# A first weight loaded ahead of two value pairs, and one batch's q turned in two transfers, in an attention-and-maxout kernel

## The chip, the cores and the metric

The kernel runs on one core of one Trainium2 chip. The metric is device time in microseconds (us) of one execution; lower is better. "Span" is the stretch that the profile covers; it is about 1.8 us shorter than the device time of the same run (405.9 for 407.72). A ratio is the mean time of one kernel's fast runs over that of the other's of the same rounds, so it is not quite the ratio of the medians quoted beside it. Where a landing is given, it is the issue time plus the time to landing that the DMA view rounds to a tenth, so it is good to 0.05 us. A "stand" is a time in which PE stands idle.

## The reference, cut to what matters

```python
# batch 8, heads 8, sequence 1024, head_dim 64; k_proj 64
k_proj = einsum('ks,bhsd->bhkd', E, k);  v_proj = einsum('ks,bhsd->bhkd', F, v)
attn   = softmax(q @ k_proj.T / 8)
x      = (attn @ v_proj), heads side by side          # 8192 x 512
out    = max(x @ w1, x @ w2, x @ w3) @ w_out          # d_ff 768
```

## The kernel before

Each batch needs three loads (q, k, v; float32 in memory, cast to bf16 by the transfer), a projection of k and of v, q with head_dim on the partitions (`qT`), scores, the softmax, and `xT`, which the three weights multiply. The program order on each engine is fixed by hand. TensorE (PE) does the weight matmuls without a break, and the attention of the next batch lies between them.

Three places matter. The loads of the start, all on one queue in this order:

```python
load_q(LO, ...); load_kv(1, LO); load_q(HI, ...); load_kv(1, HI)   # q and k of batch 0
load_kv(2, slice(0, 2)); load_kv(2, slice(2, 4))                   # v pairs 0 and 1
...
load_kv(2, V2)                 # v pair 2
load_w(0, slice(0, 2))         # first half of the first weight
load_kv(2, V3)                 # v pair 3
...                            # rest of the weights, rest of q, w_out, then batch 1's q, k, v
```

The end of the start, and the first weight. `v_pair(g)` projects a pair of heads of v (8 matmuls), `x(g)` is its product with the attention (4 matmuls) and its scaling into `xT` on VectorE (DVE), `idle(n)` is n dummy matmuls; `z(g)` is the softmax sums of a pair and their inverse. (`at`, in the diff below, issues nothing: it only sets the time that the program keeps for choosing banks.)

```python
v_pair(1); z(2); z(3); x(1)
v_pair(2)
idle(2)
x(2)
idle(1)
...
for ct in range(4):            # up_first: 24 matmuls of the first weight, ct by ct
    for jt in range(6):
        up_mm(...); then((0, ct, jt))     # v_pair(3) after (0, 1, 2), x(3) after (0, 1, 5)
```

And batch 1's q. `qd` repacks q on DVE in four copies and turns it with one transposing transfer, on the queue of SyncE (SP). In the plan, `kproj`, `kt` and `vproj` project k, turn it, and project v; `sc` is the scores of a pair of heads and their exp, `za` its sums, its product with v and its scaling into `xT`; `qp` turns q on PE, `ld` issues a batch's loads:

```python
def qd(b):
    def f():
        q_p = att.tile([P, NPAIR, SI, 2, D], BF16, name="q_p", bufs=1)
        for g in range(NPAIR):
            copy("v", q_p[:, g]..., qkv[b][0][:, 2 * g:2 * g + 2], (), 0.43)
        qTs[b] = att.tile([P, NPAIR * SI, P], BF16, name="qT")
        last_T[b] = nc.sync.dma_start_transpose(out=qTs[b], in_=q_p...)
    return f

# plan of batch 0: (chunk, step): what follows that step; steps 0 to 5 are 12 weight matmuls each
(0, 6): [za(0, 1, *c1), sc(0, 3, *c1)],
(0, 7): [za(0, 2, *c1)],
(0, 8): [za(0, 3, *c1), qd(1)],
(1, 0): [kproj(1)],
(1, 1): [kt(1)],
(1, 2): [sc(1, 0), sc(1, 1), vproj(1), ld(2)],    # first scores of batch 1
(1, 3): [za(1, 0), sc(1, 2)],
(1, 4): [za(1, 1), sc(1, 3)],
(1, 5): [za(1, 2)],
(1, 7): [za(1, 3)],
```

The softmax here doesn't subtract the row's maximum and nothing guards it: scores larger than these inputs give would overflow.

## Time and profile before

| | before |
|---|---|
| device time, three timed runs | 409.61, 409.81, 410.21 us |
| device time of the profiled run | 407.72 us |
| PE busy, share of the span | 394.5 us, 97% |
| largest wait of PE | 2.7 us, for qT of batch 1 |

From the page of the kernel before: the busy line, the granted clock in 40 slices (tenths of full speed), and the chain of work that ended last, by engine.

```profile
PE 394.5 (97%) x2376; PEld 178.5 (44%) x2376; DVE 200.1 (49%) x309; ACT 191.1 (47%) x278; POOL 31.4 (8%) x44
PEclk9999999999999999999999999999999999999999
PE 87%; DMA 6%; ACT 2%; DVE 1%; POOL 1%; issue 1%; DVEq 0%; ACTq 0%; POOLq 0%
```

PE bounds the kernel, so only time in which PE stands can be won. The timeline of PE at the end of the start shows where it stands. Columns: start us, length us, engine, line, operation, output<-inputs, partitions, shape, count, and in brackets how long PE was idle before and what ended the idling.

```profile
17.25 0.30 PE L220 MATMUL banks<-pT,vp 64*64 64x256 bf16 x4
18.21 0.61 PE L422 MATMUL banks<-v_t,efT 128*128 128x128 bf16 x8 [0.65 <-DMA v_t<-in_v_dram]
18.65 0.59 PE L377 MATMUL banks<-warm 128*128 128x512 bf16 x2
19.20 0.30 PE L220 MATMUL banks<-pT,vp 64*64 64x256 bf16 x4
19.44 0.39 PE L377 MATMUL banks<-warm 128*128 128x512 bf16 x1
19.98 2.12 PE L497 MATMUL banks<-xT,w_sb 128*128 128x512 bf16 x9 [0.15 <-DMA w_sb<-in_moe_w_dram]
```

PE waits for v pair 2, works on it, fills up with dummies, and waits for the weight. The second place is batch 1's first scores, again in the timeline of PE; below it, the issues on the SP queue, where the 7.66 us are the time that the issue took.

```profile
52.63 2.75 PE L497 MATMUL banks<-xT,w_sb 128*128 128x512 bf16 x12
58.12 0.63 PE L200 MATMUL banks<-qT,kpT 64*64 64x512 bf16 x8 [2.73 <-DMA qT<-q_p]
...
43.77 0.35 SPq L606 DMA_DIRECT2D out_dram<-o_sb  x1
48.34 7.66 SPq L329 DMA_TRANSPOSE qT<-q_p  x1
```

### The profile page before, as it was taken

The numbers are of one execution on the slowest core, as the hardware profiler recorded it, in microseconds if no ns is written. First come the engines' busy times: TensorE is split into PE (matmuls) and PEld (weight loads), VectorE is DVE, ScalarE is ACT, GpSimd is POOL, SyncE is SP. The second block draws the span as 40 slices with busy tenths as digits, with TensorE's granted clock in tenths as the row PEclk, the third lists the DMA queues.
The fourth block names the chain that finished last, engine by engine and source line by source line (L and its number), as shares of the span: only waits on it lengthen the run. The fifth ranks groups of instructions, "written<-read, shape, count | busy, mean of one in ns | idle before, by whom it ended". The sixth has DMA issues, their size and how long they took to land.

```text
span 405.9 us, 5916 instructions
## 1 busy us (share of the span) xinstructions
PE 394.5 (97%) x2376; PEld 178.5 (44%) x2376; DVE 200.1 (49%) x309; ACT 191.1 (47%) x278; POOL 31.4 (8%) x44
## 2 busy tenths in 40 slices
PE   7899979999999999999999999999999999999996
PEld 3444433444444535444544445444544444444443
DVE  2447736462655537627353655626464363525251
ACT  2612429724763266555544555437535555432322
POOL 7440020002000100200200002000000000000000
PEclk9999999999999999999999999999999999999999
DMA  9999999948927994891798119950510202020202
GB/s 156 207 206 206 231 190 187 226 105 114 254 47 208 168 246 105 138 244 33 213 186 172 52 32 235 205 152 2 139 70 1 103 2 103 2 103 0 105 0 104
DMA packets 62635, 53.33 MB, mean 131 GB/s; under 512 B 30096, under 2 KB 58256, under 8 KB 62608
## 3 DMA queue, kind: packets, MB, share of 16 engines
q0 software_dynamic: 28512, 28.31, 43.7%
q1 hardware_dynamic: 33872, 24.25, 19.1%
q10 hardware_dynamic: 224, 0.39, 0.4%
q8 instruction: 18, 0.29, 0.3%
q14 instruction: 9, 0.07, 0.1%
HBM read 57.15 MB, written 16.78 MB: 182 GB/s over the span
## 4 chain that ended last, share of the span: by engine, by line
PE 87%; DMA 6%; ACT 2%; DVE 1%; POOL 1%; issue 1%; DVEq 0%; ACTq 0%; POOLq 0%
PE banks L497 58%; PE banks L592 19%; PE banks L220 4%; DMA w_sb<-in_moe_w_dram 3%; PE banks L284 3%; DMA qT<-q_p 2%; PE banks L200 2%; ACT pT L211 1%; ACT zl L233 1%; DVE xT L250 1%; ACT zi L239 1%; POOL v_t L147 1%; DMA out_dram<-o_sb 0%; DVE hs L507 0%; POOL k_t L147 0%
## 5 line engine op out<-in xcount | busy, mean ns | idle before, releaser
L497 PE MATMUL banks<-xT,w_sb 128*128 128x512 bf16 x1152 | 257.2, 379 | 0.2 <-DMA w_sb<-in_moe_w_dram 0.2
L497 PEld LDWEIGHTS <-w_sb 128*128 128x128 bf16 x1152 | 109.6, 98 | 136.5 <-issue 9.4
L557 DVE TENSOR_TENSOR m<-banks,h1s 128x512 f32<-128x512 f32 x90 | 62.0, 689 | 83.8 <-ACT h1s L553 52.5
L553 ACT COPY h1s<-banks 128x512 f32<-128x512 f32 x90 | 52.5, 583 | 90.0 <-PE banks L497 88.0
L592 PE MATMUL banks<-wout_sb,hT 128*128 128x512 bf16 x378 | 85.6, 379 | 0.1
L250 DVE TENSOR_TENSOR xT<-banks,zi 128x1024 bf16<-128x1024 f32 (+1 forms) x36 | 39.8, 1106 | 76.9 <-ACT zi L239 55.5
L507 DVE TENSOR_TENSOR hT<-banks,m 128x512 bf16<-128x512 f32 x90 | 62.3, 692 | 10.1 <-DVE m L557 0.5
L99 ACT COPY o_sb<-banks 128x512 f32<-128x512 f32 (+1 forms) x60 | 34.9, 581 | 52.9 <-PE banks L592 52.9
L592 PEld LDWEIGHTS <-hT 128*128 128x128 bf16 x378 | 36.0, 98 | 45.4 <-issue 2.8
L233 ACT ACTIVATE zl<-banks 128x1024 f32<-128x1024 f32 (+1 forms) x36 | 33.5, 931 | 29.5 <-PE banks L220 27.9
L211 ACT ACTIVATE pT<-banks 128x1024 bf16<-128x1024 f32 (+1 forms) x36 | 33.2, 931 | 13.5 <-PE banks L200 13.5
L239 ACT ACTIVATE zi<-zl 128x1024 f32<-128x1024 f32 (+1 forms) x36 | 34.6, 962 | 1.1
L189 POOL DMA_DIRECT2D q_t<-in_q_dram x7 | 6.2, 880 | 205.4 <-DMA qT<-q_p 142.9
L200 PE MATMUL banks<-qT,kpT 64*64 64x512 bf16 (+1 forms) x144 | 13.7, 358 | 3.2 <-DMA qT<-q_p 2.7
L220 PE MATMUL banks<-pT,ones 64*64 64x512 bf16 (+1 forms) x144 | 13.9, 375 | 0.7 <-DVE xT L250 0.3
L284 PEld LDWEIGHTS <-efT 128*64 128x64 bf16 x256 | 12.8, 110 | 4.0 <-issue 3.6
L220 PE MATMUL banks<-pT,vp 64*64 64x512 bf16 (+1 forms) x144 | 13.3, 355 | 0.1
L99 DVE CAST vp<-banks 64x256 bf16<-64x256 f32 (+1 forms) x18 | 7.1, 396 | 10.2 <-ACT vp L99 6.9
L220 PEld LDWEIGHTS <-ones 64*64 64x64 bf16 x144 | 4.5, 103 | 14.6 <-issue 13.5
L99 ACT CAST vp<-banks 64x256 bf16<-64x256 f32 x14 | 5.1, 365 | 12.0 <-PE banks L284 11.8
L377 PE MATMUL banks<-warm 128*128 128x512 bf16 x26 | 9.2, 480 | 1.2 <-DVE warm L170 1.2
L99 DVE COPY q_p<-q_t 128x1024 bf16<-128x1024 bf16 x28 | 10.0, 419 | 0.0
(46 smaller groups left out, 97.4 us busy)
## 6 DMA issues: line engine op xcount, KB each, us to landing
out_dram<-o_sb SPq DMA_DIRECT2D x30, 512.0 KB, 3.0
q_t<-in_q_dram POOLq DMA_DIRECT2D x7, 1024.0 KB, 9.5
k_t<-in_k_dram POOLq DMA_DIRECT2D x7, 1024.0 KB, 13.8
v_t<-in_v_dram POOLq DMA_DIRECT2D x7, 1024.0 KB, 18.5
w_sb<-in_moe_w_dram POOLq DMA_DIRECT2D x5, 384.0 KB, 12.3
k_t<-in_k_dram POOLq DMA_DIRECT2D x2, 512.0 KB, 8.8
v_t<-in_v_dram POOLq DMA_DIRECT2D x4, 256.0 KB, 11.5
wout_sb<-in_moe_w_out_dram POOLq DMA_DIRECT2D x1, 768.0 KB, 16.0
```

The lines of the kernel that those rows point to most:

```text
L99: done = {"v": nc.vector.tensor_copy, "s": nc.scalar.copy, "g": nc.gpsimd.tensor_copy}[eng](out=o, in_=i)
L211: nc.scalar.activation(out=pTs[b, g, lo], in_=t, func=AF.Exp, scale=scale)
L220: nc.tensor.matmul(out=t[hp * HALF:(hp + 1) * HALF, c, 0:nsi * HALF], lhsT=w(rows, hp), rhs=p[rows, hp, :], start=True, stop=True,)
L233: nc.scalar.activation(out=zl, in_=t, func=AF.Ln)
L239: nc.scalar.activation(out=zi, in_=zl, func=AF.Exp, scale=-1.0)
L250: nc.vector.tensor_tensor(out=xTs[b][:, g, lo:lo + nsi, :].rearrange("a (c s) p -> a c (s p)", c=2), in0=t, in1=zi, op=ALU.mult,)
L284: nc.tensor.matmul(out=t[hh * HALF:(hh + 1) * HALF, 0:width], lhsT=efT[:, si, (kv - 1) * KP:kv * KP], rhs=qkv[b][kv][:, heads[hh], si, :], ...
L497: nc.tensor.matmul(out=h, lhsT=w_sb[i][:, ct, jt * P:(jt + 1) * P], rhs=xTs[b][:, ct, ch * SPC:(ch + 1) * SPC, :], start=(ct == first), st ...
L507: nc.vector.tensor_tensor(out=o, in0=h, in1=other, op=ALU.max)
L553: nc.scalar.copy(out=h1s, in_=h[0][0])
L557: nc.vector.tensor_tensor(out=m12, in0=h[1][0], in1=h1s, op=ALU.max)
L592: nc.tensor.matmul(out=o_ps, lhsT=hTs[b, ch][:, jt, tt * P:(tt + 1) * P], rhs=wout_sb[:, jt, :], start=(jt == 0), stop=(jt == NJT - 1),)
```

## The change

It means to take both stands away. The first weight comes ahead of the last two v pairs, whose work then lies between weight matmuls. Batch 1's q is repacked one step sooner and turned in two halves, so that the first scores need wait for one half only. F's load also moves from the ACT to the SP queue, and batch 0's second q repacking moves by two matmuls.

```diff
-    nc.scalar.dma_start(out=ef_f[KP:P], in_=F)
+    nc.sync.dma_start(out=ef_f[KP:P], in_=F)
...
+    load_w(0, slice(0, 2))
     load_kv(2, V2)
-    load_w(0, slice(0, 2))
     load_kv(2, V3)
...
-    def qd(b):
+    def qd(b, parts=1):
...
+            n = NPAIR // parts
+            for lo in range(0, NPAIR, n):
+                for g in range(lo, lo + n):
+                    copy( ... )
+                last_T[b] = nc.sync.dma_start_transpose(
+                    out=qTs[b][:, lo * SI:(lo + n) * SI, :],
+                    in_=q_p[:, lo:lo + n].rearrange("p g si h d -> p (g si h d)"),
+                )
...
-    at(16.7)
-    v_pair(2)
-    idle(2)
-    x(2)
     idle(1)
-    at(18.4)
+    at(17.4)
...
-                (0, 7): [za(0, 2, *c1)],
-                (0, 8): [za(0, 3, *c1), qd(1)],
+                (0, 7): [qd(1, 2), za(0, 2, *c1)],
+                (0, 8): [za(0, 3, *c1)],
...
-                    (0, 1, 2): [lambda: v_pair(3), ld(1)],
-                    (0, 1, 5): [lambda: x(3)],
-                    (2, "a", 1): [qp(0, (0, 1), *c1)],
+                    (0, 0, 5): [lambda: v_pair(2)],
+                    (0, 1, 2): [lambda: x(2)],
+                    (0, 1, 5): [lambda: v_pair(3), ld(1)],
+                    (0, 2, 2): [lambda: x(3)],
+                    (2, "a", 2): [qp(0, (0, 1), *c1)],
```

More of the change, by code (lines that the diff above doesn't have):

```diff
@@ L317, in qp @@
         return f
-    def qd(b):
+    def qd(b, parts=1):
         def f():
             q_p = att.tile([P, NPAIR, SI, 2, D], BF16, name="q_p", bufs=1)
-            for g in range(NPAIR):
-                copy(
-                    "v", q_p[:, g].rearrange("p si h d -> p h si d"),
-                    qkv[b][0][:, 2 * g:2 * g + 2], (), 0.43,
-                )
-            qTs[b] = att.tile([P, NPAIR * SI, P], BF16, name="qT")
-            last_T[b] = nc.sync.dma_start_transpose(
-                out=qTs[b], in_=q_p.rearrange("p g si h d -> p (g si h d)")
-            )
+            qTs[b] = att.tile([P, NPAIR * SI, P], BF16, name="qT")
+            n = NPAIR // parts
+            for lo in range(0, NPAIR, n):
+                for g in range(lo, lo + n):
+                    copy(
+                        "v", q_p[:, g].rearrange("p si h d -> p h si d"),
+                        qkv[b][0][:, 2 * g:2 * g + 2], (), 0.43,
+                    )
+                last_T[b] = nc.sync.dma_start_transpose(
+                    out=qTs[b][:, lo * SI:(lo + n) * SI, :],
+                    in_=q_p[:, lo:lo + n].rearrange("p g si h d -> p (g si h d)"),
+                )
         return f
```

## The prediction

> **What bounds the kernel now.** TensorE: the page has it busy 394.5 of 405.9 us (97%) at a granted clock of 0.999; the chain of waits is 87% PE. The waits of PE are small: 2.7 us for qT of batch 1, 0.7 us for v_t, 0.2 us for w_sb, and about 2.7 us in the first microseconds, which the change does not touch. At most some 4 us are in reach.
>
> **Start.** In the timeline PE finishes the second value product near 17.5 us, waits 0.65 us for the third v pair (landed 18.15), does its matmuls, three dummies and a product, then waits for the first weight piece (issued 7.03, 12.9 to landing: 19.93). The POOL queue's landings come in order of issue, so swapping the two puts the weight at about 18.15 + 1.8 - 1.3 = 18.6 us and the v pair at 19.9. Six weight matmuls (0.22 us apart) fill 18.6 to 19.95; the value work then lies between weight matmuls. The first weight's 24 matmuls end at 25.6 us instead of 26.0, with perhaps 0.2 us of waiting for the last xT. The second weight lands at 24.96, the rest of q at 32.26, the last weight at 33.7, as before (same bytes ahead of them); the q transposes (before at 32.35, after waiting for a max) stand two matmuls later and meet q as it lands. Gain about 0.4 us, at most 0.8; the DMA is full here, which caps it.
>
> F moves from the ACT to the SP queue, issued 0.58 us later. The Trainium skill (Trainium Kernel Development and Optimization, Key Constraints) says all queues share the same 16 DMA engines and a further issuer saves only issue time; E and F landed at 5.4 and 6.3 us. I expect F within 0.4 us of that, hidden by the five dummies before the first k projection, which waits for k.
>
> **Batch 1's q.** Before: four copies on DVE, 46.89 to 48.31, one transfer issued at 48.34 (issue 7.66 us), landed 58.07; PE stood from 55.39 to 58.12. After: the copies follow the second o_sb copy, from about 43.3 (q landed 42.6); the first half's transfer starts near 44.1, the second near 48, landed by 54. The first scores need only the first half. PE arrives near 55.0, so the 2.73 us go entirely. The 1.42 us of copies delay xT of pairs 2 and 3 to about 45.4 and 46.7; they are needed near 46.3 and 47.8, and the banks come free in time.
>
> **What it collides with.** The first transfer now overlaps batch 1's k load (42.6 to 47.65). Before, v took 6.85 us beside the transfer instead of the 5.05 that k took. I estimate k 1 us later, 48.6, against PE's arrival at 48.5: a new wait of 0.1 to 0.5 us.
>
> **Sum.** 409.81 - 0.4 - 2.7 + 0.2 = about 406.9 us, 0.7% less. Range 405.9 to 408.4. Faster by over 2%: 0.01; within 2%: 0.98; slower by over 2%: 0.01.
>
> **Right if** the waits of PE for qT vanish, the first weight matmul starts near 18.6, the first qT transfer is issued near 44, and PE busy falls by only about 1 us while the span falls about 3.
>
> **Wrong if** (a) transfer and k load slow each other, so that PE waits 1 us or more at batch 1's k projection, or v arrives late at its projection near 55.5; (b) DVE waits for q_t at 43.3 and holds xT up; (c) the weight lands no earlier than 19.5; (d) the unmoved landings of weights, q or w_out absorb the start's gain: then about 407.3.

## The result, and the profile after

The kernel after takes 406.51 us (median of 4 runs, 406.15 to 406.83) against 409.9 (4 runs, 409.61 to 410.21): ratio 0.9917, 95% interval 0.99 to 0.9934. The forecast of 406.9 and its direction hold. The steps behind it do not, and the traces say so at once. The same lines of the page of the kernel after:

```profile
PE 391.0 (97%) x2330; PEld 178.2 (44%) x2374; DVE 199.9 (49%) x309; ACT 190.9 (47%) x278; POOL 31.6 (8%) x44
PEclk9999999999999999999999999999999999999999
PE 83%; DMA 10%; ACT 2%; issue 1%; POOL 1%; DVE 1%; ACTq 0%; POOLq 0%
```

The span is 405.1 us, only 0.8 less than in the trace before, though the timed runs differ by 3.4. (Part of the fall in PE busy is that the trace lacks some matmul records: 2330 for 2374 weight loads.) The end of the start, in the timeline of PE of the kernel after; the line of x2 has a record missing:

```profile
18.04 0.39 PE L380 MATMUL banks<-warm 128*128 128x512 bf16 x1
18.98 1.47 PE L496 MATMUL banks<-xT,w_sb 128*128 128x512 bf16 x6 [0.55 <-DMA w_sb<-in_moe_w_dram]
20.28 0.61 PE L425 MATMUL banks<-v_t,efT 128*128 128x128 bf16 x8
20.95 0.59 PE L496 MATMUL banks<-xT,w_sb 128*128 128x512 bf16 x2
21.47 0.30 PE L220 MATMUL banks<-pT,vp 64*64 64x256 bf16 x4
21.71 0.82 PE L496 MATMUL banks<-xT,w_sb 128*128 128x512 bf16 x3
22.57 0.61 PE L425 MATMUL banks<-v_t,efT 128*128 128x128 bf16 x8
```

The weight matmuls begin a microsecond sooner, and the value work lies among them as planned. Batch 1's scores and the SP queue of the kernel after:

```profile
52.86 2.75 PE L496 MATMUL banks<-xT,w_sb 128*128 128x512 bf16 x12
57.41 0.63 PE L200 MATMUL banks<-qT,kpT 64*64 64x512 bf16 x8 [1.80 <-DMA qT<-q_p]
...
43.91 0.36 SPq L605 DMA_DIRECT2D out_dram<-o_sb  x1
44.58 12.49 SPq L331 DMA_TRANSPOSE qT<-q_p  x2
```

The first half was issued 3.8 us sooner than the whole had been, yet it landed at 57.38, only 0.7 us sooner, and PE still stands for 1.80 us. So this pair of traces accounts for 0.8 us of the gain. The rest had to be found.

### The profile page after: what moved, and what is told of

It is laid out like the page before. It is cut to its first block, busy times and chain, and to the rows that moved or that the text cites. A ratio compares the mean times of both kernels' runs of the same rounds, so it can differ in the third digit from the quotient of the medians.

```text
span 405.1 us, 5869 instructions
## 1 busy us (share of the span) xinstructions
PE 391.0 (97%) x2330; PEld 178.2 (44%) x2374; DVE 199.9 (49%) x309; ACT 190.9 (47%) x278; POOL 31.6 (8%) x44
## 4 chain that ended last, share of the span: by engine, by line
PE 83%; DMA 10%; ACT 2%; issue 1%; POOL 1%; DVE 1%; ACTq 0%; POOLq 0%
PE banks L496 55%; PE banks L591 19%; PE banks L220 4%; DMA q_t<-in_q_dram 3%; DMA qT<-q_p 3%; DMA w_sb<-in_moe_w_dram 3%; PE banks L284 3%; PE banks L200 2%; ACT pT L211 1%; ACT zl L233 1%; DVE xT L250 1%; ACT zi L239 1%; DMA out_dram<-o_sb 0%; POOL k_t L147 0%; POOL q_t L152 0%
## 5 line engine op out<-in xcount | busy, mean ns | idle before, releaser
L284 PE MATMUL banks<-k_t,efT 128*64 128x256 bf16 (+1 forms) x144 | 8.7, 263 | 1.3 <-DMA k_t<-in_k_dram 1.2
```

Of the source, the lines that this page charges most:

```text
L284: nc.tensor.matmul(out=t[hh * HALF:(hh + 1) * HALF, 0:width], lhsT=efT[:, si, (kv - 1) * KP:kv * KP], rhs=qkv[b][kv][:, heads[hh], si, :], ...
```

## The experiments

All outputs were correct. Kernels ran beside eleven runs of the kernel before; their medians were 410.19 (chip of the first four kernels), 409.34 (next four) and 409.31 (last four).

**1. `a_before`: the kernel before, unchanged.**

> The kernel before, unchanged, to learn how far its profiled run of 407.7 us stands for its timed runs of 409.6 to 410.2. Theory A (the one trace of before is typical, the 2 us are the profile's own offset): ratio 1.000 within 0.002, and a new trace with a span near 406, PE waiting 2.7 us for qT and not at all for batch 1's k. Theory B (that trace was a quick execution; the DMA landings of the start vary by about a microsecond from run to run): a new trace with later landings than 9.7 us for the first k, and a longer span, near 408.

Five fast runs: 408.04, 408.06, 409.23, 409.28, 410.28; median 409.23, ratio 0.997 (0.9948 to 0.9992) against the very same program. So an interval can miss by 0.3%, and a difference under about 1 us needs a trace. The run that was profiled (513.58 us, clock 0.754) serves for nothing. The numbers lie in two groups about 1.2 us or more apart, and the first trace of before (407.72) belongs to the quicker one: Theory B, in its first half. The record gives each run's mean granted clock too: 0.998 and 0.999 in the two quick runs, 0.994 to 0.995 in the other three.

**2. `b_start`: the start part alone.** Edit: the load order, the start sequence, the `up_first` places and the later q step of the diff above; F and `qd` as before.

> The start alone: first weight loaded ahead, value pairs between its matmuls, first q step later; F still on the ACT queue, batch 1's q repacked as before. Theory A (prediction): 0.4 us less, ratio 0.999, as the start is held by landings. Theory B (the start is worth most of the 3.4 us, because the typical before stands longer there than its trace showed): 2 to 3 us less, ratio 0.993 to 0.995.

Median 409.80, ratio 0.999 (0.9973 to 1.0006). Theory B of this run falls. Whether it gives 0.4 us or nothing is settled below with twelve traces.

**3. `c_q`: the q part alone.** Edit: `qd(b, parts)` and the two lines of the plan.

> Batch 1's q alone: copies a step sooner, two transfers; start as before. Theory A (prediction): 2.5 us less, ratio 0.994, wait of PE for qT gone. Theory B (the trace after: the transfer moves hardly any packets while the k and v loads run and ends with the v load): qT wait falls by about 1 us only, a wait for k of about 1 us appears, total within 0.5 us of before, ratio 0.999 to 1.001.

Median of five fast runs 407.09, ratio 0.9922 (0.9906 to 0.9939), nearly the whole gain. Its trace is slow (418.7 us) and not used; run 9 repeats it.

**4. `d_f`: F on the SP queue alone.**

```diff
-    nc.scalar.dma_start(out=ef_f[KP:P], in_=F)
+    nc.sync.dma_start(out=ef_f[KP:P], in_=F)
```

> Only F's load moved to the SP queue. Prediction: nothing, ratio 1.000 within 0.001. Rival (in the trace after, the first k landed 0.6 us later than in that of before, and everything behind it too; F's move would be the cause): the first k lands 0.6 us later in this trace, and the time rises by 0.3 to 0.6 us.

Runs of 407.03, 407.22, 407.53 and of 409.20, 409.47, 409.50: two groups again, their means 2.1 us apart. The ratio, 0.9954, comes from how many runs fell in each, and with run 1 in mind I draw no gain from it. The rival falls: the first k landed at 9.81 us in this trace, against 9.71 in that of before and about 10.3 to 10.81 in the other fast traces with F on the ACT queue.

This trace, of a run of the slower group, shows what can separate the groups. The windows view, with windows laid on the edges of the clock records; columns: stretch, length, busy us of each engine (instructions), granted clock of PE, DMA share, GB/s. First `d_f`, then the first trace of before. The clock records of `d_f` begin and end at 7.16, 58.36, 61.77 and 406.52 us, whole multiples of 3.413 us apart; before has none between 5.56 and 404.92, and its edges are counted on from these two in the same steps.

```profile
54.95:58.36 3.41, 0.86 (x11) 0.24 (x8) 1.12 (x2) 0.00 (x0) 0.00 (x0) 1.00 1.22 338
58.36:61.77 3.41, 3.19 (x26) 1.72 (x20) 0.37 (x1) 0.73 (x2) 2.62 (x3) 0.50 0.44 47
61.77:65.18 3.41, 3.39 (x23) 1.26 (x22) 1.87 (x4) 2.98 (x4) 0.00 (x0) 1.00 1.17 181
```

```profile
53.35:56.76 3.41, 2.03 (x10) 0.81 (x9) 1.65 (x4) 0.59 (x1) 0.00 (x0) 1.00 1.29 222
56.76:60.17 3.41, 2.06 (x27) 1.21 (x27) 0.00 (x0) 0.38 (x2) 1.54 (x2) 1.00 0.61 202
```

In `d_f` the stand of 2.55 us fell into one window of 3.41 us, PE was busy for 0.86 us of it, and the clock was halved for the whole next window, 0.4 us after the scores began. In the first trace of before an edge, at 56.76, cut the stand of 2.73 us in two, PE was busy for 2.03 and 2.06 us of the windows, and the clock stayed. The Trainium skill describes this (TensorE: Matmul & The Clock Gate, Part 1: The HAM clock gate): the array's clock is halved after an idle window of 4096 cycles at 1.2 GHz, 3413 ns, and the window runs freely, not from the kernel's start. The trace agrees on both: the half-clock stretch lasts 3.41 us, and the edges stand elsewhere in every run. It differs in one point: the window need not be idle, busy for a quarter is little enough. The mean clock does not sort all runs, though: the two quickest of `d_f` (407.03 and 407.22) have 0.994 and 0.995, as the slow ones have. Where their clock dropped, and why it cost them nothing that shows, is not known.

The cost: from the start of the scores to the end of the program's fifth `h1s` copy on ScalarE (the second after the scores) takes 7.53 us in the trace of before, 9.11 in `d_f`, 9.04 in `b_start` (whose scores also ran at half clock) and 8.91 in `e_one` (run 6). A drop there costs about 1.5 us on top of the stand. The next run tests this by itself.

**5. `k_fill`: the stand filled with dummies.** The stand stays, the idling goes.

```diff
-                (1, 2): [sc(1, 0), sc(1, 1), vproj(1), ld(2)],
+                (1, 2): [lambda: idle(11), sc(1, 0), sc(1, 1), vproj(1), ld(2)],
```

> The kernel before with 11 dummy matmuls (about 2.4 us of PE time) set just before batch 1's first scores, where PE otherwise stands for qT; nothing else changed, and qT lands no sooner. Theory C (in most executions of before the granted clock halves for 3.41 us right after that stand, as the traces of d_f and b_start show and the first trace of before does not; that costs about 1.7 us more than the stand itself): 1.5 to 2 us less than before, about 408.2, the fast runs in one group rather than spread from 408.0 to 411.5, and a clock of 1.00 in the stretch after 58 us. Rival (the clock event is harmless, only the landing of qT counts): unchanged, or slower by up to 0.3 us, ratio 1.000 to 1.001.

All six runs lie between 408.07 and 408.40. The kernel before, in the same rounds: five runs from 407.65 to 408.42 and six from 409.34 to 410.26. In these rounds the mean clock sorts the runs of before exactly: 0.999 in the five, 0.994 to 0.996 in the six; in `k_fill` it is 0.999 or 1.000 in all but the profiled run, whose one drop lies in the start. So the slower group is gone and the quicker one is where it was: filling the stand with useless work wins what the clock drop cost, and no more. Its trace has no drop after the scores, which start at 58.44, and the 7.53 us are back:

```profile
56.38:59.79 3.41, 3.41 (x34) 1.72 (x32) 0.48 (x1) 0.00 (x0) 1.04 (x2) 1.00 0.80 244
59.79:63.21 3.42, 3.37 (x25) 1.39 (x21) 1.96 (x4) 2.87 (x5) 1.58 (x2) 1.00 0.84 101
```

Against the slower group's 409.7 the gain is 1.4 us, just short of the 1.5 to 2 forecast; against the mean of before it is 0.7 us (ratio 0.9983, 0.9962 to 1.0003), as half of those runs were quick.

**6. `e_one`: the kernel after, with one transfer.**

```diff
-                (0, 7): [qd(1, 2), za(0, 2, *c1)],
+                (0, 7): [qd(1), za(0, 2, *c1)],
```

> The kernel after, but batch 1's q turned in one transfer, still issued a step sooner. Theory (the transfer's 256-byte packets pass at about 150 a us while loads run, and only the end of the v load frees them; two halves bring nothing, since both landed within 1.8 us of each other): same as after, 406.5 within 0.5. Prediction's view (scores need only the first half, which lands early): 1 us or more slower than after.

My theory of that moment missed: median 409.68, ratio 1.0007 (0.9979 to 1.0035). Without the split nothing is left of the gain. PE and the SP queue in the trace of `e_one`:

```profile
58.65 1.07 PE L200 MATMUL banks<-qT,kpT 64*64 64x512 bf16 x8 [3.02 <-DMA qT<-q_p]
...
45.35 11.23 SPq L331 DMA_TRANSPOSE qT<-q_p  x1
```

Issued 3.0 us sooner than before, it landed at 58.65, if anything later (58.04 before), and the clock dropped. The reason is in the DMA view. Two queues of the kernel after from 50 to 52 us, q0 being the loads and q1 the transfer (packets, MB, share of 16 engines' time), then q1 of the kernel before from 56 to 57 us, when the loads had ended:

```profile
q0 software_dynamic: 303, 0.31, 91.0%
q1 hardware_dynamic: 304, 0.08, 29.9%
```

```profile
q1 hardware_dynamic: 1132, 0.29, 128.0%
```

Beside a load the two queues pass as many packets, 304 to 303 in 2 us. The Trainium skill (DMA: Bandwidth & Descriptors, Queues, rings and completion order) states that an engine goes round its queues a packet at a time; a packet there holds several descriptors, and whether the packets of the profile are the same is not shown. The equal counts agree with equal turns, and here the turns are unequal in size: the transfer's packets hold 256 bytes, the load's 1024. So it passes 152 packets a us, and 1132 alone. The whole transfer is 1 MB, 4096 packets; most of it goes through once batch 1's v load is done. An early transfer takes turns from the loads: v landed between 55.56 and 56.22 us in the six traces with an early issue, and between 54.44 and 55.68 in the six with a late one (`a_before` and the slow trace of `c_q` left out), on average about 1 us later. An early issue also starts the packets less early than it seems. In the trace of after the transfer was issued at 44.58 but moved its first 256-byte packet at 49.46, against 48.34 and 51.69 in before: 3.8 us sooner in issue, 2.2 in packets. The output write issued just ahead of it on the same queue moved its own packets from 47.41 to 50.16; that the transfer waited behind it was not tested. The engines are full, so what the transfer gains by starting sooner, the load ahead of the fast stretch gives back.

**7. `g_after_late`: the kernel after, batch 1's attention one step later.** PE then reaches the scores when qT is there.

```diff
-                (1, 0): [kproj(1)],
-                (1, 1): [kt(1)],
-                (1, 2): [sc(1, 0), sc(1, 1), vproj(1), ld(2)],
-                (1, 3): [za(1, 0), sc(1, 2)],
-                (1, 4): [za(1, 1), sc(1, 3)],
-                (1, 5): [za(1, 2)],
+                (1, 1): [kproj(1)],
+                (1, 2): [kt(1)],
+                (1, 3): [sc(1, 0), sc(1, 1), vproj(1), ld(2)],
+                (1, 4): [za(1, 0), sc(1, 2)],
+                (1, 5): [za(1, 1), sc(1, 3)],
+                (1, 6): [za(1, 2)],
```

> The kernel after, with batch 1's k projection, k turn, scores and all but the last of its exp-and-value steps one matmul step (2.6 us) later, so that PE reaches the scores after qT has landed near 57.4. Theory: no wait for qT at all, another 1.5 to 1.8 us less than after, about 404.8. Rival (the wait only moves to the later steps, to xT or to the v projection): same as after.

Median 405.40 (404.88 to 407.11), ratio 0.9918 (0.9894 to 0.9942), the lowest of all medians. PE in its trace no longer waits for qT:

```profile
58.31 0.63 PE L200 MATMUL banks<-qT,kpT 64*64 64x512 bf16 x8
```

A wait of 0.4 us for a bank that VectorE frees late has come up at a following output step, so some 1.4 of the 1.8 us should remain; the medians differ by 1.0 to 1.1, less than the 1.5 to 1.8 that was forecast.

**8. `h_before_late`: the kernel before, with the same later steps and nothing else.**

> The kernel before with only those steps of batch 1 one matmul step later: same transfer at the same time, start unchanged. Theory C: the wait of 2.7 us falls to nearly nothing and no clock drop follows, so 4 us less than before, about 405.7; it would beat the kernel after without any of its changes. Rival: the wait moves elsewhere; 408 or more.

Median 406.62 (406.51 to 407.19), ratio 0.9944 (0.9923 to 0.9965). PE waits 0.22 us for qT and the clock stays at full speed. The expected 405.7 was 0.9 us too hopeful; the new 0.4 us wait for a bank is part of the difference. A move in the plan, without a transfer touched, thus brings a time close to that of the kernel after. In the same rounds the mean of `g_after_late` is still 1.1 us lower (405.62 and 406.70); of this 0.5 us stands at the start of the scores in the two traces (58.31 and 58.80), the wait for qT included; the rest is not explained.

**9. `c_q_again`: the q part alone, for a fast trace.**

> The q part alone once more, for a trace in the fast state (the first fell in the slow one). Theory D (two halves let the first scores start when the first half lands, about 1 us before a single transfer would, which shortens PE's stand to under 2 us, and the granted clock then does not drop): qT wait 1.5 to 2 us against 2.5 to 3.0, no half-clock stretch near 58 us, about 407. Prediction's view (the wait goes entirely, no other effect): qT wait under 0.3 us.

Runs of 405.98 to 407.86, median 407.28, ratio 0.9948 (0.9927 to 0.9969). Line of PE's waits from 14 to 70 us in its trace:

```profile
PE banks L200 <- DMA qT<-q_p: 1.4, 1, 1.4
```

No half-clock stretch follows in this trace (one of the three other runs, 407.47, has a mean clock of 0.994, so its clock dropped somewhere). The prediction's view (under 0.3 us) falls; Theory D holds, with a wait a little under its 1.5 to 2 us.

**10. `f_split_late`: the kernel before, with two transfers at the old step.**

```diff
-                (0, 8): [za(0, 3, *c1), qd(1)],
+                (0, 8): [za(0, 3, *c1), qd(1, 2)],
```

> The kernel before with batch 1's q turned in two transfers, but at the old step. Theory D, the split is what counts: the first half lands near 57.2 instead of 58.3, the wait is about 1.5 to 2 us, mostly no clock drop, 1.5 to 3 us less than before. Rival, the earlier issue counts as much (the first half needs the 2.3 us of packet time that it gained beside the loads): first half lands at 58 or later, wait as before, clock drop, within 0.7 us of before.

Median 406.68 (405.50 to 406.77), ratio 0.9932 (0.9915 to 0.9949): the gain of the whole change. Its PE and SP lines, and the window of the clock in which the stand falls:

```profile
57.28 0.63 PE L200 MATMUL banks<-qT,kpT 64*64 64x512 bf16 x8 [1.35 <-DMA qT<-q_p]
...
48.09 8.78 SPq L331 DMA_TRANSPOSE qT<-q_p  x2
```

```profile
54.21:57.62 3.41, 2.06 (x16) 0.83 (x14) 1.38 (x2) 0.59 (x1) 0.00 (x0) 1.00 1.29 191
```

The first half landed at 57.19 and the second at 58.98, 1.8 us apart, which is 2048 packets at 1132 a us. The scores start on the first half, the stand is 1.35 us, and a stand that short leaves PE busy enough (2.06 us) even where one window holds all of it.

**11. `a_after`: the kernel after again.**

> The kernel after again, beside the others: 406.5 within 0.6, no half-clock stretch near 58 us, qT wait 1 to 2 us. If its start part is worth what was predicted, 0.4 us less than the q part alone; if nothing, equal to it within 0.3.

Median 406.40 (405.74 to 407.10), ratio 0.9931 (0.9916 to 0.9946); wait 1.4 us for qT, no clock drop. It equals `f_split_late` of the same rounds (means 406.40 and 406.48). Of the two forecasts for the start neither fits: the q part alone, `c_q_again`, has a mean of 407.10, 0.7 us more, but from four runs spread over 1.9 us; the first `c_q` had nearly the ratio of the whole change (0.9922 and 0.9917). The timed runs leave a few tenths open, so the start is judged by traces below.

**12. `m_spread`: as `g_after_late`, the last two steps further on.**

```diff
-                (1, 6): [za(1, 2)],
-                (1, 7): [za(1, 3)],
+                (1, 7): [za(1, 2)],
+                (1, 8): [za(1, 3)],
```

> The kernel after with batch 1's steps later as in g_after_late, and the last two exp-and-value steps one further step on, so that the first output step does not wait 0.4 us for a bank that VectorE frees late. If that wait is all that g lost: 0.3 to 0.4 us less than g, about 405.0. If the last xT comes too late for batch 1's first matmuls instead: 0.5 us or more above g.

Median 405.69 (405.54 to 406.06), ratio 0.9915 (0.99 to 0.993), 0.7 us under `a_after` of the same rounds by the means (405.74 and 406.40). Against g, of another submission, no difference can be claimed: the expected 0.3 to 0.4 us is below what separates submissions. In its trace the 0.4 us wait is gone, but PE waits 0.7 us for the last `xT` at the first matmuls that need it (77.12 us): the wait has moved.

**The start part, from twelve traces.** PE's first weight matmul, and the start of the first `o_sb` copy on DVE, which all twelve share after the start; us.

```
start as before   first weight  first o_sb     start changed    first weight  first o_sb
before               19.98        40.85        after               18.98        41.00
d_f                  20.29        40.91        b_start             19.72        41.60
k_fill               20.99        41.60        e_one               19.22        41.10
h_before_late        20.64        41.45        g_after_late        19.38        41.25
c_q_again            20.60        41.43        a_after             19.32        41.20
f_split_late         20.13        41.27        m_spread            19.56        41.44
mean                 20.44        41.25        mean                19.36        41.27
```

The first weight starts 1.1 us sooner, and 20 us later nothing is left; the first k landed at the same time in both columns on average (10.3 us). With six traces a side that spread by up to 0.75 us, a gain below some 0.3 us (an estimate from this spread) could still hide. The gain is lost inside the first weight: from its first matmul to the last of the six `hs` copies that take its results away takes 6.52 us in the trace of before and 7.78 in that of after (starts of the two). In between now lie a further v pair (8 matmuls, 0.45 us), a further product with its pause (0.33 us), a pause of 0.20 us before the last v pair's matmuls, and one of 0.28 us for the last xT: 1.26 us together, the whole difference. Before, PE did that pair and that product while it waited for the weight anyway; they cost nothing there. What is won in landing is about what the moved work costs in its new place.

Also, chance moves this point by up to 0.75 us between runs of equal kernels: compare before with `k_fill`, equal up to there. It follows the loads: the first k landed at 9.71 in the one and at 10.81 in the other.

## Why the prediction was right or wrong, point by point

- **The time (406.9 predicted, 406.51 measured), the direction and the range** were right, the number by luck: in the q part too large a cut of the wait and a clock cost that was left out nearly cancelled, at 2.7 us predicted. Of the "right if" list the main point failed, as the wait for qT did not vanish.
- **"The 2.73 us go entirely": wrong.** The stand is 1.80, 1.42 and 1.39 us in the three fast traces with the q part as changed, so 0.9 to 1.3 us of the 2.73 went. The mistake was to give each half of the transfer half of the issue time seen before, as if its rate were its own. Beside loads it moves 152 packets a us and alone 1132, so it ends by when the loads end; and its first packet moved only at 49.46, not near 44.1.
- **The earlier step** was half of the argument; it brings nothing measurable (`e_one`, and `f_split_late` against `a_after`). The split does all of it, by letting the first scores start 1.8 us before the second half lands.
- **A term not in the sum: the clock.** The stand of 2.5 to 3 us halved the granted clock for 3.41 us in many runs, at about 1.5 us each time; with 1.4 us of stand no trace shows it. Filling the stand (`k_fill`) shows the same without a faster transfer. The sign was there: a profiled run 2 us faster than all timed runs. Shorter stand, about 1.3 us, and clock, about 1.5 us in the runs that dropped, come near the 2.8 us between the means of `f_split_late` (406.48) and of before in its rounds (409.31). How often before drops can be read from the mean clocks, though not where in the run: 26 of its 33 runs beside the experiments have 0.996 or less (11 of 11, 6 of 11 and 9 of 11 by submission), and these are slower than the rest of their submission by 1.6 us on average in the second and 1.0 us in the third.
- **The start's 0.4 us: mis-sized.** The weight landed at 18.90 to 19.67 us, not 18.6, on average 1.0 us sooner and not 1.3. With the moved work and the wait for xT it measured 0.0 at the first output copy, give or take 0.3; `b_start` says 0.999 with 1 inside its interval, which fits 0.4 us as well as nothing. Point (d) of "wrong if" named the place, but the landings of later weights are not the cause; the moved work is.
- **The new wait for batch 1's k, 0.1 to 0.5 us: nearly nothing.** k landed at 49.14 us in the trace of after as PE reached it, and at 47.89 in that of `a_after`. The predicted cause, the transfer beside the k load, did not come about: no packet of the transfer moved before 49.46, and `f_split_late`, with a late transfer, also had its k late, at 49.4. The later v load was the larger collision, and there too v came in time.
- **xT and the banks around the earlier copies: right.** No new wait of PE appears there.
- **F: right.** It landed at 5.88 us in the kernel after, against 6.34, and no delay follows. Whether its move is worth a few tenths is open; the timed runs of `d_f` and `a_before` do not agree well enough to tell.

## What to carry to other kernels

A wait of the matrix engine can cost more than its length: if the same kernel's runs fall into two groups, look at the granted clock just after the largest wait, and test by filling the wait with dummies. The transfer of small packets beside large loads got its turns here, not its share of bytes, so issuing it sooner moved little; cut it so that the consumer needs only its first part, or move the consumer (one plan step did more than the transfer's timing). And work done inside an unavoidable wait cost nothing here: moving it out to end the wait sooner must win more than the work costs where it goes.

## What the Trainium skill lacked or had wrong

- TensorE: Matmul & The Clock Gate, Part 1: it says that the clock is halved after an idle window, with idle gaps over about 3.4 us to be avoided. Here a stand of 2.5 us was enough, in windows with 0.86 us (`d_f`) and 0.94 us (`b_start`) of 3.41 busy; at 2.03 and 2.06 us busy the clock stayed. In `k_fill` a window of the start with 1.38 us busy was followed by a drop as well, as its two lines show (the stretch before, and the one at half clock). With 1.66 us busy the clock stayed at full speed in two windows of the start, 7.40 to 10.81 us in `b_start` and 4.21 to 7.62 in `m_spread`; where between 1.38 and 1.66 the limit lies, no run shows. Below, `k_fill`, then `b_start`.

```profile
8.60:12.01 3.41, 1.38 (x21) 0.81 (x20) 0.43 (x2) 0.00 (x0) 0.59 (x2) 1.00 1.24 188
12.01:15.42 3.41, 3.41 (x37) 1.49 (x34) 0.92 (x2) 1.99 (x4) 1.04 (x2) 0.50 1.24 205
```

```profile
7.40:10.81 3.41, 1.66 (x23) 0.82 (x19) 1.16 (x3) 0.58 (x1) 1.12 (x2) 1.00 1.25 187
10.81:14.23 3.42, 3.14 (x53) 1.74 (x53) 1.21 (x3) 1.59 (x3) 1.10 (x2) 1.00 1.25 205
```

- The same page does not say that one wait in the middle of a kernel can split the times of identical runs into groups: the runs of before beside `k_fill` fell into two groups 1.6 us apart by their means, and the mean clock sorts them. That this goes by where the free-running window lay rests on four traces with a stand of 2.5 us or more: three dropped, and in the fourth an edge cut the stand in two.
- DMA: Bandwidth & Descriptors, Queues, rings and completion order: the turns by packet are there, but not what they do to a transposing transfer on chip. In the profile its packets are of 256 bytes, so beside a load with 1024-byte packets it falls from 1132 to 152 packets a us, from about 290 to 39 GB/s.
- TensorE: Matmul & The Clock Gate, Part 1, tells of a limit of 13/16 of the clock (0.8125) once three cores of a die run dense matmuls. Here single executions of a one-core program ran at a mean granted clock of 0.754 (513.58 us, in `a_before`) and 0.949 (418.7 us, in `c_q`); what the other cores of the chip did then is not in these profiles, neither figure is 0.8125, and it stays open whether this is that limit or another.
